# Last-8 keys of a segment packed four heads to a row quadrant, and the output projection in two column halves

## The chip, the cores and the metric

The kernel runs on one core of one Trainium2 chip. The metric is the device time of one execution, in microseconds (us). The engines are named as the profile names them: PE is the matrix engine (PEld its weight loads), DVE the vector engine, ACT the scalar engine, POOL the general engine, SP the engine that issues most DMAs. PSUM is the accumulator memory of PE; it has eight banks of 128 partitions by 2 KB.

## The reference

The model mixes a recurrent attention branch and a small network with a gate. There are 2048 tokens of 512 values, 32 heads of 128, and 64 segments of 32 tokens. Each segment sees 8 memory rows and its own 32 tokens, and the first 8 output rows of a segment are the next segment's memory, so the segments form a chain.

```
for s in range(n_seg):
    h = concatenate([mem, x[:, 32*s:32*s+32]])        # 40 rows
    q, k, v = h@Wq, h@Wk, h@Wv                        # 32 heads of 128
    scores = where(mask, q k^T * scale, -1e9)          # memory rows see all
    o = einsum('bhte,hed->btd', softmax(scores) v, Wo)
    mem = o[:, :8]; outs.append(o[:, 8:])
g = sigmoid((x * gate_w).sum(-1))
return g * a + (1 - g) * (gelu(layernorm(x) @ w1 + b1) @ w2 + b2)
```

## The kernel before

A first stage (lines up to L188) computes the network branch for all tokens and keeps it in SBUF; it ends at about 111 us. After it, a main loop goes over the 64 segments, with two more turns at the end to drain.

**Rows.** PE works on 32 columns of stationary operand at a time, four such quarters beside each other (`tile_position`). A segment has 8 memory rows, 24 tokens that share a quarter with them (the *ride* rows) and the last 8 tokens (the *left* rows). The left rows of four segments, a group T of 128 tokens, are projected together one group ahead: `left_qk` and `left_v` (L265, L276 on the operand `GL`) give `QL`, `KL` and `VL` of a group. Four segments, si = 0 to 3, make a group, and the program repeats with a group's period.

**One turn of the loop**, in PE's order: the q and k projections in five PSUM banks (`qk_unit`, L265 on `hT`), v with one and a half banks (L276), the scores (L413 for 32 keys, L417 for the left keys), the rest of v, the sums of the memory queries' weights (L533, L534), five units of filler, the weighted values of the memory queries, `Um` (L427, L431), the sums of the token queries (L544, L545), two units of filler, the output projection `wo_unit` (L287, 32 matmuls of 512 columns into one bank `wp`), the weighted values of the token queries of the segment before, `Ux` (the same lines L427, L431), a unit of filler, the transposed memory `aT` (L575), the mask of the next segment (L404) and a last unit of filler. The output projection of turn s takes the memory rows of segment s and the ride rows of segment s-2.

**Filler** is the work that no segment waits for at once: `left_qk`, `left_v` of the next group, `wo_left` (the output projection of the left rows), the assembly of the output (L361, L370, L375). A unit is four matmuls of 512 columns or the like, and there are nine a turn.

**Order.** From the first mask on the order is written out by hand (`manual_schedule`): each engine runs its instructions as the loop issues them. DVE and ACT casts that follow filler are put in the lists `dve_q` and `act_q`, and `flush` issues them. Before that point a scheduler orders the work. The seven banks of pool `pb` go round: a new tile waits until the reader of the tile seven allocations before is done. In SBUF, `wsb` (L565, L566) holds the projection of a turn, and `aT` of the next turn reads all of its 512 columns, so the chain of the recurrence is wp, the DVE cast of columns 0 to 255, the ACT cast of columns 256 to 511, aT, `hT` (L576), q.

`ux_out` (L485) casts the four tiles of `Ux` with ACT into `UTT`, whose last axis is the segment in the group, so that each value lands four elements from its neighbour. `Um` lands there by L548, two casts on DVE and two on ACT.

Of the kernel before, what the change touches and what calls it, by code (L numbers as in the profile page):

```python
# [23 lines left out]
def kernel(ctx, tc, A_x, A_mem0, A_Wq, A_Wk, A_Wv, A_Wo, A_seg_len, B_x, B_w1, B_b1, B_w2, B_b2, gate_w, out):  # L24
# [189 lines left out]
    nc.gpsimd.memset(UTT[:], 0.0)  # L214
# [8 lines left out]
    for i in range(SPT):  # L223
        nc.gpsimd.memset(SelL[i][:], 0.0)
        nc.vector.tensor_copy(out=SelL[i][:, RIDE:32], in_=Sel[:, i:32:SPT])
# [3 lines left out]
    for si in range(SPT):  # L229
        for g in range(4):  # L230
            q = slice(32 * g, 32 * g + 32)
            for (c0, c1) in ((0, M), (EW - LEFT, EW)):
                sl = MkA[q, si, c0:c1]
                nc.gpsimd.memset(sl, 0.0)
                nc.gpsimd.affine_select(out=sl, in_=sl, pattern=[[0, c1 - c0]], compare_op=ALU.is_ge,
                                        fill=MASK_NEG, base=-LEFT * si, channel_multiplier=1)
            sl = MkA[q, si, 0:M]
            nc.gpsimd.affine_select(out=sl, in_=sl, pattern=[[0, M]], compare_op=ALU.is_ge,
                                    fill=MASK_NEG, base=LEFT * si + LEFT - 1, channel_multiplier=-1)

            sl = MkA[q, si, EW - LEFT:EW]
            nc.gpsimd.affine_select(out=sl, in_=sl, pattern=[[1, LEFT]], compare_op=ALU.is_ge,
                                    fill=MASK_NEG, base=LEFT * si, channel_multiplier=-1)

            sl = MkA[q, si, 2 * M:2 * M + RIDE]
# [4 lines left out]
    ps = loop.enter_context(tc.tile_pool(name="ps", bufs=1, space=PSUM))  # L250
    cw = loop.enter_context(tc.tile_pool(name="cw", bufs=2))
# [32 lines left out]
    def wo_unit(bk, lhs, u):  # L284
        for (j, i) in HORD[4 * u:4 * u + 4]:
            g = i % 4
            nc.tensor.matmul(bk[32 * g:32 * g + 32, :], lhsT=lhs(i, j), rhs=Wo_sb[:, 4 * i + j, :],  # L287
                             start=(j == 0 and i < 4), stop=(j == 3 and i >= NG - 4), tile_position=(0, 32 * g))

    xTs, GLs, wsbs, wsbLs = {}, {}, {}, {}  # L290
# [30 lines left out]
    def left_qk(T, t, hf):  # L321
        h0, h1 = HF[hf]
        bk = bank([P, 512])
        for kc in range(KC):
            qk_unit(bk, GLs[T], t, h0, h1, kc)
            if kc < KC - 1:
                yield
        dst = (QL, KL)[t][T % 2]

        def ev():  # L330
            nc.gpsimd.tensor_copy(out=dst[:, h0:h1, :], in_=qk_tr(bk, h0, h1))
# [12 lines left out]
    def wo_left(T):  # L344
        bk = bank([P, Dm])
        for u in range(8):
            wo_unit(bk, lambda i, j: UTT[:, i, j, 32:40, :].rearrange("p c i -> p (c i)"), u)
# [32 lines left out]
    def filler(T):  # L380

        if T + 1 < NT:
            for hf in range(2):
                for t in range(2):
                    yield from left_qk(T + 1, t, hf)
            for vb in range(2):
                yield from left_v(T + 1, vb)
        if T >= 1:
            yield from out_units(T - 1)
        elif NT > 2:  # L390
            x_tr(2, x_load(2))
            yield
# [9 lines left out]
    def mask_mm(s):  # L402
        S = ps.tile([P, NG, EW], FP32, tag="S", name="S")
        nc.tensor.matmul(S[:], lhsT=ident[:], rhs=MkA[:, s % SPT, :].unsqueeze(1).to_broadcast([P, NG, EW]),  # L404
# [3 lines left out]
    def scores(S, s, i0, i1):  # L408
        T = s // SPT
        for i in range(i0, i1):  # L410
            for j in range(4):
                h = 4 * i + j
                nc.tensor.matmul(S[32 * j:32 * j + 32, i, M:M + 40], lhsT=KT[:, h, :], rhs=QT[:, h, :],  # L413
                                 start=False, stop=True, skip_group_check=True, tile_position=(0, 32 * j))
            for j in range(4):
                h = 4 * i + j
                nc.tensor.matmul(S[32 * j:32 * j + 32, i, :].rearrange("p (a b) -> p a b", b=8)[:, 0:7:6, :],  # L417
                                 lhsT=KL[T % 2][:, h, :], rhs=QT[:, h, :].rearrange("p (a b) -> p a b", b=8)[:, 0:5:4, :],
                                 start=False, stop=True, skip_group_check=True, tile_position=(0, 32 * j))

    def av(U, n, s, V, Pt, c_main, c_left, u0):

        T = s // SPT
        for i in range(NG):
            for j in range(4):
                q = slice(32 * j, 32 * j + 32)
                nc.tensor.matmul(U[j][:, i, :], lhsT=V[q, i, :], rhs=Pt[q, i, c_main:c_main + n],  # L427
                                 start=(i == 0), stop=False, skip_group_check=True, tile_position=(32 * j, 0))
            for j in range(4):
                q = slice(32 * j, 32 * j + 32)  # L430
                nc.tensor.matmul(U[j][:, i, u0:u0 + 8], lhsT=VL[T % 2][q, i, :], rhs=Pt[q, i, c_left:c_left + 8],  # L431
# [27 lines left out]
    S_next = mask_mm(0)  # L459
    Es, Rs, Pxs, Vs, Uxs = {}, {}, {}, {}, {}  # L460
    fill, left = iter(()), iter(())

    def run_fill(n):
        for _ in range(n):
            if next(left, 0) == 0 and (T + 1 < NT or si >= 2):
                next(fill, None)
# [15 lines left out]
    def ux_out(s):  # L482
        T, si = divmod(s, SPT)
        for j, U in enumerate(Uxs.pop(s)):
            nc.scalar.copy(out=UTT[:, :, j, M:40, si], in_=U[:])  # L485

    for s in range(nseg + 2):
# [5 lines left out]
        if si == 1 and 1 <= T < NT:  # L493
            left = wo_left(T - 1)
        if live:
# [3 lines left out]
            if s >= 1:  # L499
                x_mul(s - 1)  # L500
            flush(dve_q)
            if s + 1 < nseg and (s + 1) // SPT in xTs:
                prep_h(s + 1)
            if s >= 1:
                prep_q(s)
            BANKS = [(0,) + HF[0], (1,) + HF[0], (0,) + HF[1], (1, H // 2, 3 * H // 4), (1, 3 * H // 4, H)]
# [16 lines left out]
            scores(S, s, 0, NG // 2)  # L523
            scores(S, s, NG // 2, NG)
# [22 lines left out]
            for j in range(4):  # L547
                (nc.scalar.copy if j % 2 else nc.vector.tensor_copy)(out=UTT[:, :, j, 0:M, sp], in_=Um[j][:])  # L548
# [16 lines left out]
        nc.vector.tensor_copy(out=wsb[:, 0:256], in_=wp[:, 0:256])  # L565
        nc.scalar.copy(out=wsb[:, 256:512], in_=wp[:, 256:512])  # L566
# [5 lines left out]
        if s + 1 < nseg:  # L572
# [4 lines left out]
            S_next = mask_mm(s + 1)  # L577
        run_fill(1)
        if si == 1:
            for _ in left:  # L580
                pass
# [3 lines left out]
    for _ in wo_left(NT - 1):  # L585
        pass
# [137 lines left out]
```

## Time and profile before

| what | value |
|---|---|
| median of 2 runs | 979.15 us (977.44 to 980.86) |
| the profiled execution | 980.17 us, of which its span is 978.4 us |
| mean granted clock of PE | 0.98 |
| PE busy | 871.1 us (89%) |
| PEld busy | 518.0 us (53%) |
| DVE busy | 514.7 us (53%) |
| ACT busy | 525.9 us (54%) |
| POOL busy | 257.0 us (26%) |

The profile is of one execution. A row of the timeline gives the start in us, the duration in us, engine, line, operation, output and input, the shape, and the count; in brackets is the idle time of that engine just before, with what ended it. A row of the groups gives the busy sum in us and the mean of one in ns, then the idle time before them. Matmuls overlap, so a row of 16 matmuls lasts less than sixteen times the mean of one, and the last one's duration goes on after the next group has begun.

### The profile page before, as it was taken

Reading aid. Unit: us, or ns where it says so; the run is one execution under the profiler, and the core shown is the slowest. Engines: PE = TensorE matmul, PEld = TensorE weight load, DVE = VectorE, ACT = ScalarE, POOL = GpSimd, SP = SyncE. Lnnn points to the kernel's source line nnn. Section 1 sums busy time; section 2 is a strip of 40 time slices with the busy share of each in tenths; the row PEclk is TensorE's granted clock in tenths of the full one; section 3 lists DMA queues with packets and bytes.
Section 4 is the critical chain, followed back from the end, with each engine's and each line's share of the span. In section 5 each row is a group of like instructions: output and inputs, shape, how many; then the busy total and the mean of one; then the engine's idle time right before and its main releaser. Section 6 shows DMA issues by size and latency. Waiting matters only on the chain.

```text
span 978.4 us, 53663 instructions
## 1 busy us (share of the span) xinstructions
PE 871.1 (89%) x24969; PEld 518.0 (53%) x24977; DVE 514.7 (53%) x999; ACT 525.9 (54%) x1252; POOL 257.0 (26%) x599
## 2 busy tenths in 40 slices
PE   2999649998999999999999999989899999999996
PEld 1666315555555555555555555555555555555553
DVE  4721416554556555655565555555555545555553
ACT  2655324555555555555555555555555555555564
POOL 1000463222222232223222223222222222232320
PEclk9999779999999999999999999999999999999999
DMA  9960000000000000000000000000000000000000
GB/s 285 422 199 1 12 2 4 9 4 3 16 4 14 4 15 3 15 4 15 4 15 3 15 4 3 15 4 15 3 15 4 15 4 15 3 9 4 10 7 12
DMA packets 14996, 29.65 MB, mean 30 GB/s; under 512 B 1032, under 2 KB 12656, under 8 KB 13232
## 3 DMA queue, kind: packets, MB, share of 16 engines
q1 hardware_dynamic: 14592, 25.90, 7.4%
q8 instruction: 197, 3.23, 1.4%
q0 software_dynamic: 176, 0.27, 0.3%
q14 instruction: 31, 0.25, 0.1%
HBM read 24.06 MB, written 2.10 MB: 27 GB/s over the span
## 4 chain that ended last, share of the span: by engine, by line
PE 78%; ACT 11%; DVE 4%; issue 3%; POOL 2%; DMA 1%; SPq 1%; POOLq 0%; ACTq 0%; DVEq 0%
PE b L265 29%; PE b L287 16%; PE b L276 11%; ACT UTT L485 4%; PE b L427 4%; PE bp L172 4%; PE hp L178 3%; PE b L431 3%; ACT E L530 2%; DVE wsb L565 2%; ACT wsb L566 2%; PE S L417 2%; PE S L413 2%; PE b L533 1%; PE b L544 1%
## 5 line engine op out<-in xcount | busy, mean ns | idle before, releaser
L271 DVE STREAM_TRANSPOSE Tt<-b 128x512 f32<-128x512 f32 (+1 forms) x384 | 225.6, 613 | 111.3 <-PE b L265 82.7
L265 PEld LDWEIGHTS <-hT 128*32 128x32 bf16 x5120 | 144.3, 98 | 111.1 <-issue 14.4
L485 ACT CAST UTT<-b 128x256 bf16<-128x256 f32 x256 | 158.3, 822 | 10.8 <-PE b L431 10.5
L287 PE MATMUL b<-Wo_sb,UTT 128*32 128x512 bf16 x2624 | 161.5, 383 | 2.3 <-ACT UTT L485 1.6
L265 PE MATMUL b<-Wq_sb,hT 128*32 128x512 bf16 x2048 | 137.2, 388 | 18.7 <-POOL hT L396 13.5
L265 PE MATMUL b<-Wk_sb,hT 128*32 128x256 bf16 (+1 forms) x3072 | 137.4, 313 | 0.0
L276 PE MATMUL b<-Wv_sb,hT 128*32 128x512 bf16 x2048 | 134.5, 380 | 0.0
L472 POOL TENSOR_TENSOR Px<-E,R 128x256 bf16<-128x256 bf16 x64 | 43.2, 675 | 345.2 <-DVE R L549 345.2
L513 ACT CAST KT<-Tt 128x256 bf16<-128x256 f32 (+1 forms) x192 | 86.8, 476 | 57.4 <-DVE Tt L271 57.4
L549 DVE RECIPROCAL R<-b 128x256 f32<-128x256 f32 x64 | 112.0, 1750 | 4.5 <-PE b L545 4.5
L566 ACT CAST wsb<-b 128x256 bf16<-128x256 f32 x66 | 24.6, 373 | 157.7 <-DVE wsb L565 157.7
L287 PEld LDWEIGHTS <-UTT 128*32 128x32 bf16 x2624 | 73.0, 106 | 62.4 <-ACT UTT L485 3.5
L427 PEld LDWEIGHTS <-V 32*128 32x128 bf16 x4096 | 68.0, 91 | 58.1 <-DVE Pm L539 29.5
L537 DVE RECIPROCAL R<-b 128x64 f32<-128x64 f32 x64 | 35.7, 558 | 96.6 <-PE b L534 96.6
L513 POOL CAST QT<-Tt 128x512 bf16<-128x512 f32 x64 | 39.4, 616 | 172.4 <-DVE Tt L271 172.4
L431 PEld LDWEIGHTS <-VL 32*128 32x128 bf16 x4096 | 69.1, 91 | 13.4 <-issue 13.3
L548 ACT CAST UTT<-b 128x64 bf16<-128x64 f32 x128 | 28.5, 319 | 79.8 <-PE b L431 79.8
L276 PEld LDWEIGHTS <-hT 128*32 128x32 bf16 x2048 | 53.5, 96 | 25.9
L513 ACT CAST QT<-Tt 128x512 bf16<-128x512 f32 x64 | 39.6, 618 | 50.0 <-DVE Tt L271 49.4
L178 PE MATMUL hp<-yT,w_sb 128*128 128x256 bf16 (+1 forms) x352 | 53.0, 278 | 4.8 <-ACT hTm L179 3.1
L548 DVE CAST UTT<-b 128x64 bf16<-128x64 f32 x128 | 28.4, 301 | 54.0 <-PE b L431 54.0
L179 ACT ACTIVATE hTm<-hp,b_sb 128x256 bf16<-128x256 f32 (+1 forms) x88 | 40.6, 470 | 29.9 <-PE hp L178 29.8
(111 smaller groups left out, 1271.4 us busy)
## 6 DMA issues: line engine op xcount, KB each, us to landing
Wq_sb<-in_A_Wq_dram SPq DMA_DIRECT2D x4, 1024.0 KB, 13.0
Wk_sb<-in_A_Wk_dram SPq DMA_DIRECT2D x4, 1024.0 KB, 18.7
Wv_sb<-in_A_Wv_dram SPq DMA_DIRECT2D x4, 1024.0 KB, 20.2
Wo_sb<-in_A_Wo_dram SPq DMA_DIRECT2D x4, 1024.0 KB, 17.2
out_dram<-o SPq DMA_DIRECT2D x16, 128.0 KB, 1.7
xc<-in_A_x_dram SPq DMA_DIRECT2D x15, 128.0 KB, 2.3
x_all<-in_A_x_dram SPq DMA_DIRECT2D x3, 512.0 KB, 9.2
w_sb<-in_B_w_dram SPq DMA_DIRECT2D x1, 1376.0 KB
```

The costliest lines, as they stand in the source:

```text
L178: nc.tensor.matmul(hp[:rows, :], lhsT=w1_sb[:, kc, fc * P:fc * P + rows], rhs=yT[:, kc, :], start=(kc == 0), stop=(kc == KC - 1))
L265: nc.tensor.matmul(bk[32 * j:32 * j + 32, 0:n], lhsT=G[:, kc, :], rhs=W5[t][:, kc, h0:h1, j, :], start=(kc == 0), stop=(kc == KC - 1), til ...
L271: nc.vector.transpose(out=Tt[:, 0:n], in_=bk[:, 0:n])
L276: nc.tensor.matmul(bk[32 * j:32 * j + 32, :], lhsT=G[:, kc, :], rhs=Wv5[:, kc, 4 * vb:4 * vb + 4, j, :], start=(kc == 0), stop=(kc == KC - ...
L287: nc.tensor.matmul(bk[32 * g:32 * g + 32, :], lhsT=lhs(i, j), rhs=Wo_sb[:, 4 * i + j, :], start=(j == 0 and i < 4), stop=(j == 3 and i >= ...
L427: nc.tensor.matmul(U[j][:, i, :], lhsT=V[q, i, :], rhs=Pt[q, i, c_main:c_main + n], start=(i == 0), stop=False, skip_group_check=True, til ...
L431: nc.tensor.matmul(U[j][:, i, u0:u0 + 8], lhsT=VL[T % 2][q, i, :], rhs=Pt[q, i, c_left:c_left + 8], start=False, stop=True, skip_group_che ...
L485: nc.scalar.copy(out=UTT[:, :, j, M:40, si], in_=U[:])
L513: (nc.gpsimd.tensor_copy if bi == 2 else nc.scalar.copy)(out=dst, in_=Tv)
L548: (nc.scalar.copy if j % 2 else nc.vector.tensor_copy)(out=UTT[:, :, j, 0:M, sp], in_=Um[j][:])
L549: nc.vector.reciprocal(out=R[:, 8 * NG:].rearrange("p (i q) -> p i q", q=32), in_=sr[:])
L566: nc.scalar.copy(out=wsb[:, 256:512], in_=wp[:, 256:512])
```

## The change

**Left keys.** Before, each of the 32 heads has a matmul of its own for the left keys: the stationary operand is the 32 left keys of all four segments for this head, of which the mask lets 8 count. Afterwards the stationary operand holds the 8 left keys of this segment for four heads (`KL` in the order group of heads, segment, head, key), and the moving operand the two query blocks of the four heads, so that 8 matmuls of 64 columns stand for 32 of 16. Of the result only the blocks with query and key of the same head count; `MkA` masks the others and is now the same for all segments, so `mask_mm` takes no segment. The values follow: `VL` has the rows of four heads in a quarter, and in `Um` and in `Ux` 8 matmuls of 32 columns stand for 32 of 8. Main and left matmuls no longer alternate: the left ones come after all main ones.

**Values through DRAM.** The left values are cast by ACT into `vt`, written to a DRAM tile in two DMAs of a group, and read back by 16 DMAs, all issued by SP. `KL` is written by POOL in two casts of 128x256 for each bank in place of one of 128x512. `left_v` is moved ahead of `left_qk` in the filler, and `wo_left`, which had a list of its own that began in the second segment, is put behind `left_qk`.

**Output projection.** `UTT` becomes two tiles, one for even and one for odd groups, in which a value's neighbours lie beside each other: segment si uses columns 24-8si to 64-8si, and its left rows end up in columns 32 to 63. `wo_unit` runs twice over 256 columns, into two banks; DVE casts the first half between the two in program order, and ACT the second.

**Small moves.** POOL does `prep_h` and `prep_q` ahead of `x_mul`, and the flush of `dve_q` follows. The memset of `UTT` covers 2048 columns in place of 5120, and 32 small memsets of `MkA` are gone.

```diff
-    KL = [lp.tile([P, H, 32], BF16, name=f"KL{i}") for i in range(2)]
-    VL = [lp.tile([P, NG, Dh], BF16, name=f"VL{i}") for i in range(2)]
-    UTT = lp.tile([P, NG, 4, 40, SPT], BF16)
-    MkA = lp.tile([P, SPT, EW], BF16)
+    KL = [lp.tile([P, 8, SPT, 4, LEFT], BF16, name=f"KL{i}") for i in range(2)]
+    VL = [lp.tile([P, SPT, 2, Dh], BF16, name=f"VL{i}") for i in range(2)]
+    UTT = [lp.tile([P, NG, 4, 64], BF16, name=f"UTT{i}") for i in range(2)]
+    MkA = lp.tile([P, 4, EW], BF16)
...
-    nc.gpsimd.memset(UTT[:], 0.0)
+    nc.gpsimd.memset(UTT[1][:], 0.0)
...
-    def wo_unit(bk, lhs, u):
+    def wo_unit(bk, ut, c0, u, d0=0, d1=Dm):
         for (j, i) in HORD[4 * u:4 * u + 4]:
             g = i % 4
-            nc.tensor.matmul(bk[32 * g:32 * g + 32, :], lhsT=lhs(i, j), rhs=Wo_sb[:, 4 * i + j, :],
+            nc.tensor.matmul(bk[32 * g:32 * g + 32, :], lhsT=ut[:, i, j, c0:c0 + 32], rhs=Wo_sb[:, 4 * i + j, d0:d1],
...
+            if t == 0:
+                nc.gpsimd.tensor_copy(out=QL[T % 2][:, h0:h1, :], in_=Tv)
+            else:
+                for hh in range(h0 // 8, h1 // 8):
+                    r0 = 8 * hh - h0
+                    nc.gpsimd.tensor_copy(out=KL[T % 2][:, :, :, hh, :], in_=Tv[:, r0:r0 + 8, :].rearrange("p g (s c) -> p g s c", c=LEFT))
...
-        act_q.append(lambda: nc.scalar.copy(out=v_out(VL[T % 2], vb), in_=bk[:]))
+        def ev():
+            vt = cw.tile([P, 4, Dh], BF16, tag="vt", name="vt")
+            nc.scalar.copy(out=vt[:].rearrange("p i e -> p (i e)"), in_=bk[:])
+            if vb == 0:
+                vds[T] = dr.tile([P, 4, 2, Dh], BF16, tag="vd", name="vd")
+            nc.sync.dma_start(vds[T][:, 2 * vb:2 * vb + 2], vt[:].rearrange("p (a g) e -> p a g e", g=2))
+            if vb == 1:
...
+                for j in range(4):
+                    for hh in range(4):
+                        r0 = 32 * j + LEFT * hh
+                        nc.sync.dma_start(VL[T % 2][r0:r0 + LEFT].rearrange("p s g e -> p s (g e)"), src[j, hh])
...
-    def scores(S, s, i0, i1):
+    def scores(S, s):
...
+        for g in range(2):
             for j in range(4):
...
-                                 lhsT=KL[T % 2][:, h, :], rhs=QT[:, h, :].rearrange("p (a b) -> p a b", b=8)[:, 0:5:4, :],
+                                 lhsT=KL[T % 2][:, 4 * g + j, si, :, :].rearrange("p h c -> p (h c)"),
+                                 rhs=QT[:, 4 * g + j:H:8, :].rearrange("p h (a b) -> p h a b", b=8)[:, :, 0:5:4, :],
...
+        for g in range(2):
             for j in range(4):
                 q = slice(32 * j, 32 * j + 32)
-                nc.tensor.matmul(U[j][:, i, u0:u0 + 8], lhsT=VL[T % 2][q, i, :], rhs=Pt[q, i, c_left:c_left + 8],
+                nc.tensor.matmul(U[j][:, g:NG:2, u0:u0 + 8], lhsT=VL[T % 2][q, si, g, :], rhs=Pt[q, g:NG:2, c_left:c_left + 8],
...
-            nc.scalar.copy(out=UTT[:, :, j, M:40, si], in_=U[:])
+            nc.scalar.copy(out=UTT[T % 2][:, :, j, c0 + M:c0 + 40], in_=U[:])
...
-        wp = bank([P, Dm])
-        for u in range(8):
-            wo_unit(wp, lambda i, j: UTT[:, i, j, 0:32, sp], u)
-        flush(act_q, 2)
         wsb = cw.tile([P, Dm], BF16, tag="wsb", bufs=7, name="wsb")
-        nc.vector.tensor_copy(out=wsb[:, 0:256], in_=wp[:, 0:256])
-        nc.scalar.copy(out=wsb[:, 256:512], in_=wp[:, 256:512])
+        for half in range(2):
+            d = slice(256 * half, 256 * half + 256)
+            wp = bank([P, 256])
+            for u in range(8):
+                wo_unit(wp, UTT[Tp % 2], 24 - 8 * sp, u, 256 * half, 256 * half + 256)
+            if half == 0:
+                flush(act_q, 2)
+            (nc.scalar.copy if half else nc.vector.tensor_copy)(out=wsb[:, d], in_=wp[:])
```

The rows that follow are from the program's own order, of one engine each; in brackets are the engines that an instruction waits for, and the numbers behind a name tell tiles of one pool apart.

PE at the end of the output projection of a third segment (si = 2), before: `b_15386` is the bank of the projection, `b_15424` to `b_15427` are the four tiles of `Ux`.

```order
L287 MATMUL b_15386<-Wo_sb_61,UTT_1153 32x512
L427 LDWEIGHTS V_14720
L427 MATMUL b_15424<-Px_15063,V_14720 128x32
L427 LDWEIGHTS V_14720
L427 MATMUL b_15425<-Px_15063,V_14720 128x32 [waits Activation_49]
L427 LDWEIGHTS V_14720
L427 MATMUL b_15426<-Px_15063,V_14720 128x32 [waits DVE_49]
L427 LDWEIGHTS V_14720
L427 MATMUL b_15427<-Px_15063,V_14720 128x32 [waits Activation_49]
L431 LDWEIGHTS VL1_1152
L431 MATMUL b_15424<-Px_15063,VL1_1152 128x8
L431 LDWEIGHTS VL1_1152
```

The same place on PE afterwards: `b_14407` is the bank of the second half, `b_14441` to `b_14444` are the tiles of `Ux`.

```order
L291 MATMUL b_14407<-Wo_sb_61,UTT1_1154 32x256
L451 LDWEIGHTS V_13769
L451 MATMUL b_14441<-Px_14092,V_13769 128x32
L451 LDWEIGHTS V_13769
L451 MATMUL b_14442<-Px_14092,V_13769 128x32 [waits DVE_49]
L451 LDWEIGHTS V_13769
L451 MATMUL b_14443<-Px_14092,V_13769 128x32 [waits DVE_49]
L451 LDWEIGHTS V_13769
L451 MATMUL b_14444<-Px_14092,V_13769 128x32 [waits Activation_49]
L451 LDWEIGHTS V_13769
```

The second half of the projection stands directly ahead of `Ux`, the left matmuls have left the space between the main ones, and the fourth tile of `Ux` now follows an ACT reader of a half's bank rather than the reader of the whole.

ACT at the same two places. Before, `b_15302` and `b_15304` are tiles of `Um`, `wsbL` is the projection of the left rows, `wsb` that of the turn:

```order
L548 CAST UTT_1153<-b_15302 128x8x8 [waits PE_49]
L548 CAST UTT_1153<-b_15304 128x8x8 [waits PE_49]
L353 CAST wsbL_15419<-b_14831 128x512
L566 CAST wsb_15421<-b_15386 128x256 [waits DVE_49]
L485 CAST UTT_1153<-b_15424 128x8x32 [waits PE_49]
L485 CAST UTT_1153<-b_15425 128x8x32 [waits PE_49]
L485 CAST UTT_1153<-b_15426 128x8x32 [waits PE_49]
L485 CAST UTT_1153<-b_15427 128x8x32 [waits PE_49]
```

And afterwards, where `b_14407` is the second half:

```order
L570 CAST UTT1_1154<-b_14312 128x8x8 [waits PE_49]
L570 CAST UTT1_1154<-b_14314 128x8x8 [waits PE_49]
L590 CAST wsb_14372<-b_14407 128x256 [waits PE_49]
L511 CAST UTT1_1154<-b_14441 128x8x32 [waits DVE_49,PE_49,Activation_49]
L511 CAST UTT1_1154<-b_14442 128x8x32 [waits PE_49,Activation_49]
L511 CAST UTT1_1154<-b_14443 128x8x32 [waits DVE_49,PE_49]
L511 CAST UTT1_1154<-b_14444 128x8x32 [waits PE_49,Activation_49]
```

The ACT cast of `wsb` waited for DVE, which cast the other columns of the same bank first, and now waits for PE alone; the cast of `wsbL` has moved to another segment.

POOL just ahead of the loop, before (the copy of the first group's `GL` stands 80 rows earlier, directly behind the memset of `MkA`):

```order
L235 AFFINE_SELECT MkA_1154<-MkA_1154 32x8 [waits Pool_49] x2
L314 COPY GL_1493<-xT_1491 128x128 [waits DVE_49,Pool_49]
L238 AFFINE_SELECT MkA_1154<-MkA_1154 32x8 [waits Pool_49]
L242 AFFINE_SELECT MkA_1154<-MkA_1154 32x8
L238 AFFINE_SELECT MkA_1154<-MkA_1154 32x8
L242 AFFINE_SELECT MkA_1154<-MkA_1154 32x8
L235 AFFINE_SELECT MkA_1154<-MkA_1154 32x8 x2
L396 COPY hT0_1142<-xT_1480 128x4x24 [waits Pool_49]
L396 COPY hT1_1143<-xT_1480 128x4x24
```

And afterwards:

```order
L245 AFFINE_SELECT MkA_1155<-MkA_1155 32x8 [waits Pool_49]
L241 AFFINE_SELECT MkA_1155<-MkA_1155 32x8 [waits Pool_49]
L245 AFFINE_SELECT MkA_1155<-MkA_1155 32x8 [waits Pool_49]
L318 COPY GL_1453<-xT_1451 128x128 [waits DVE_49,Pool_49]
L419 COPY hT0_1142<-xT_1451 128x4x24
L419 COPY hT1_1143<-xT_1451 128x4x24
L318 COPY GL_1464<-xT_1462 128x128 [waits DVE_49]
L335 CAST QL0_1147<-Tt_1484 128x512 [waits DVE_49]
L339 CAST KL0_1149<-Tt_1504 128x32x8 [waits DVE_49]
```

Both copies of `GL` and those of `hT` now stand behind the last of `MkA`'s selects, which before lay partly behind the first and the second.

More of the change, by code (lines that the diff above doesn't have):

```diff
@@ L224 @@
         nc.gpsimd.memset(SelL[i][:], 0.0)
-        nc.vector.tensor_copy(out=SelL[i][:, RIDE:32], in_=Sel[:, i:32:SPT])
+        nc.vector.tensor_copy(out=SelL[i][:, RIDE:32], in_=Sel[:, LEFT * (SPT - 1 - i):LEFT * (SPT - i)])
     nc.gpsimd.memset(MkA[:], 0.0)
-    for si in range(SPT):
+    for hh in range(4):
         for g in range(4):
@@ L382, in filler @@
         if T + 1 < NT:
+            for vb in range(2):
+                yield from left_v(T + 1, vb)
             for hf in range(2):
@@ L385, in filler @@
                     yield from left_qk(T + 1, t, hf)
-            for vb in range(2):
-                yield from left_v(T + 1, vb)
         if T >= 1:
+            yield from wo_left(T - 1)
             yield from out_units(T - 1)
@@ L522 @@
                 v_unit(vb1, hc, 1, kc)
[L523 to L524 removed]
+            scores(S, s)
             for kc in range(2, KC):
@@ L576 @@
             nc.vector.tensor_copy(out=hn[:, :, 0:M], in_=aT[:])
-            S_next = mask_mm(s + 1)
+            S_next = mask_mm()
         run_fill(1)
-        if si == 1:
-            for _ in left:
-                pass
         if si == SPT - 1:
```

57 lines of the change are left out of this document (27 added, 30 removed).

## The prediction

> **What bounds the kernel now.** I read the page first, for the busy shares and the chain that ended last.
>
> ```profile
> span 978.4 us, 53663 instructions
> PE 871.1 (89%) x24969; PEld 518.0 (53%) x24977; DVE 514.7 (53%) x999; ACT 525.9 (54%) x1252; POOL 257.0 (26%) x599
> PE 78%; ACT 11%; DVE 4%; issue 3%; POOL 2%; DMA 1%; SPq 1%; POOLq 0%; ACTq 0%; DVEq 0%
> ```
>
> PE holds 78% of the chain, ACT and DVE 15% between them: less PE work and shorter hand-overs can both count. Next the windows of one group of four segments, from mask to mask (columns: us, then busy us of each engine, granted clock).
>
> ```profile
> 500.38:551.73 51.35, 48.28 (x1525) 28.74 (x1523) 29.01 (x54) 29.08 (x72) 14.47 (x29) 1.00 0.03 9
> 229.40:234.60 5.20, 5.20 (x88) 2.66 (x84) 2.55 (x5) 2.21 (x4) 1.17 (x3) 0.67 0.01 3
> ```
>
> A group takes 51.35 us, of which PE is idle for 3.07. The second row is one of three spots with a low clock. Then the timeline of a first segment (si = 0) of that group, into the second.
>
> ```profile
> 500.92 1.05 PE L265 MATMUL b<-Wq_sb,hT 128*32 128x512 bf16 x16 [0.18 <-ACT UTT L485]
> 501.78 1.05 PE L265 MATMUL b<-Wk_sb,hT 128*32 128x512 bf16 x16
> ...
> 503.50 1.06 PE L265 MATMUL b<-Wk_sb,hT 128*32 128x256 bf16 x32
> 504.38 1.48 PE L276 MATMUL b<-Wv_sb,hT 128*32 128x512 bf16 x24
> ...
> 505.53 0.58 ACT L519 CAST V<-b 128x512 bf16<-128x512 f32 x1
> 505.67 0.21 PE L413 MATMUL S<-QT,KT 128*32 128x40 bf16 x4
> ...
> 506.17 0.62 PE L276 MATMUL b<-Wv_sb,hT 128*32 128x512 bf16 x8
> 506.50 0.28 ACT L530 ACTIVATE E<-S 128x128 bf16<-128x128 f32 x1 [0.39 <-PE S L417]
> ...
> 508.26 0.18 PE L427 MATMUL b<-Pm,V 32*128 32x8 bf16 x4
> ...
> 508.70 0.20 PE L431 MATMUL b<-Pm,VL 32*128 32x8 bf16 x4
> 508.97 0.45 DVE L548 CAST UTT<-b 128x64 bf16<-128x64 f32 x2 [0.85 <-PE b L431]
> 509.51 1.90 PE L287 MATMUL b<-Wo_sb,UTT 128*32 128x512 bf16 x32
> 511.46 0.42 DVE L565 CAST wsb<-b 128x256 bf16<-128x256 f32 x1 [0.47 <-PE b L287]
> 511.92 0.37 ACT L566 CAST wsb<-b 128x256 bf16<-128x256 f32 x1 [2.46 <-DVE wsb L565]
> 512.19 2.47 ACT L485 CAST UTT<-b 128x256 bf16<-128x256 f32 x4
> 512.35 0.24 PE L575 MATMUL b<-Sel,wsb 128*128 128x8 bf16 x4
> 512.45 0.35 PE L404 MATMUL S<-MkA,ident 128*128 128x448 bf16 x1
> 512.99 0.40 PE L265 MATMUL b<-Wq_sb,GL 128*32 128x512 bf16 x4 [0.19 <-ACT UTT L485]
> 513.55 1.05 PE L265 MATMUL b<-Wq_sb,hT 128*32 128x512 bf16 x16 [0.17 <-ACT UTT L485]
> ```
>
> The chain of the recurrence runs through every row: scores, exponentials (ACT waits for the last score), Um, its casts, the projection, the DVE cast, then the ACT cast in series, aT, mask, q. Whatever PE does less of ahead of a hand-over shortens the turn. The third segment (si = 2) ends worse:
>
> ```profile
> 534.77 1.90 PE L287 MATMUL b<-Wo_sb,UTT 128*32 128x512 bf16 x32
> 536.73 0.42 DVE L565 CAST wsb<-b 128x256 bf16<-128x256 f32 x1 [0.53 <-PE b L287]
> 537.18 0.37 ACT L566 CAST wsb<-b 128x256 bf16<-128x256 f32 x1 [2.57 <-DVE wsb L565]
> 537.61 0.17 PE L427 MATMUL b<-Px,V 32*128 32x32 bf16 x1 [0.81 <-ACT wsb L566]
> 538.29 2.46 ACT L485 CAST UTT<-b 128x256 bf16<-128x256 f32 x4 [0.74 <-PE b L431]
> 539.07 0.24 PE L575 MATMUL b<-Sel,wsb 128*128 128x8 bf16 x4 [0.53 <-ACT UTT L485]
> ```
>
> Here the fourth tile of Ux waits for the bank of the projection, and aT for the bank of Ux's first tile: 2.40 us from the projection's end (536.67) to aT, against 0.94 in the first segment (511.41 to 512.35).
>
> **The change part by part**, per group of four segments. The groups by form give the durations that the timeline lacks (busy sum in us, mean in ns).
>
> ```profile
> L485 ACT CAST UTT<-b 128x256 bf16<-128x256 f32 x256 | 158.3, 822 | 10.8 <-PE b L431 10.5
> L566 ACT CAST wsb<-b 128x256 bf16<-128x256 f32 x66 | 24.6, 373 | 157.7 <-DVE wsb L565 157.7
> L287 PEld LDWEIGHTS <-UTT 128*32 128x32 bf16 x2624 | 73.0, 106 | 62.4 <-ACT UTT L485 3.5 <-issue 1.7 <-DVE UTT L548 1.6
> ```
>
> *Scores.* 64 matmuls take 505.67 to 506.17, 0.50 us, 7.8 ns each, so the 32 left ones cost 0.25. Eight of 64 columns replace them. By issue they cost 8 × 7.8 = 0.06; by columns too, since the projection's 512 columns take 1.90/32 = 59 ns, which makes 7.4 ns for 64. Gain 0.18 a turn, 0.72 a group. The bound on the other side is nothing: if their scattered columns cost 31 ns each, or if ACT, which has the V cast until 506.11, is late instead.
>
> *Um.* 60 starts from 508.26 to 508.70 give 7.3 ns a matmul; 24 go, 0.17 a turn, 0.68 a group, on the path since the L548 casts and the projection follow at once. Ux loses 24 as well, which counts below.
>
> *Projection in halves.* No row has narrow projection matmuls; the nearest is K with 256 columns: 32 of them, weight loads included, take 503.50 to 504.38, 0.88 us, against 0.86 for 16 of 512 (500.92 to 501.78). Doubling the loads costs 0.02 per 32, so 0.04 a turn, +0.16 a group. In K's rows the four quarters in a row load the same hT columns, as the projection's do not, so the other bound is a rival below.
>
> The Trainium skill, "TensorE: Matmul & The Clock Gate", section "The mechanism", says that a weight load overlaps running matmuls only where its row group differs, and here all loads use all rows; its section "LDWEIGHTS (loading the stationary operand)" gives columns/1.2 ns, an estimate of 27 ns for 32 columns. By that page the 32 added loads cost 0.85 a turn and the sum ends near 983; K's 27.5 ns for load and matmul together speak against it.
>
> *Hand-over of wsb, si = 0 and 3.* DVE's 0.42 and the 0.04 behind it leave the path, since DVE casts the first half while PE does the second; at most 0.46. PE itself still has Ux (shorter by 0.17) and a filler unit (0.21 of PE's time by 0.86/4) ahead of aT, so I take 0.30, twice: 0.60.
>
> *si = 2.* The fourth tile of Ux now waits for ACT's half alone. After the projection's end: ACT 0.06 + 0.37, then 0.06 to PE, 0.49; the rest of Ux, now 537.61 to 538.25 or 0.64, less 0.19, 0.94; the first Ux cast 0.04 + 0.37 + 0.06, 1.41 in place of 2.40. Gain 1.0, if that cast takes what ACT takes for a 128x256 tile into neighbouring columns (L566, 373 ns) and not the 822 of L485, whose target had a stride of four. With the old 0.78 it is 1.76: gain 0.64.
>
> The Trainium skill, "SBUF — State Buffer", section "Door 1: The DMA port swizzle (why `[64,N]` ≈ `[32,N]`)", says that two hits per 16-byte line give full bandwidth, so bf16 may stride by up to 8 for free; by that rule L485 would gain nothing. The two rows of the trace, 822 against 373 for like tiles from PSUM, speak against it but differ in more than the stride.
>
> *si = 1.* In the changed program aT waits here for Ux's first tile, as si = 2 did: 0.42 for ACT's half, 0.47 for the cast, 0.9 in all, against 0.94 now; nothing, or +0.3 with slow casts. Its q projection starts 1.10 after the mask (512.45 to 513.55) against 0.54 in the first segment, behind L485; with four casts in some 1.5 in place of 2.47 I take 0.45 of the 0.56. The wait of the token sums for an Um cast moves from si = 2 to si = 1, at no change.
>
> *Values through DRAM.* 18 DMAs a group on SP, whose queue is otherwise stores and loads of x. left_v comes first in the filler, so they have three segments, some 38 us. Hidden. POOL's extra casts lie in its 37 idle us of 51.
>
> *Start.*
>
> ```profile
> 111.23 4.37 POOL L214 MEMSET UTT<- 128x5120 bf16 x1 [106.62 <-ACT c_all L188]
> 117.48 0.14 POOL L234 MEMSET MkA<- 32x8 bf16 x2
> 117.59 1.90 PE L265 MATMUL b<-Wq_sb,GL 128*32 128x512 bf16 x16 [3.22 <-POOL MkA L234]
> 124.39 0.35 PE L404 MATMUL S<-MkA,ident 128*128 128x448 bf16 x1
> 138.24 1.90 PE L265 MATMUL b<-Wq_sb,hT 128*32 128x512 bf16 x16 [13.49 <-POOL hT L396]
> 138.61 0.19 POOL L242 TENSOR_SCALAR_AFFINE_SELECT MkA<-MkA 32x8 bf16<-32x8 bf16 x1
> 144.39 0.19 PE L413 MATMUL S<-QT,KT 128*32 128x40 bf16 x4
> ```
>
> GL now comes after all of MkA's selects, the last of which ended at 138.80. But the memset of UTT is shorter by 4.37 × 3/5 = 2.6, 16 pairs of small memsets go (0.14 and a start each, some 3.5), and GL and hT (some 0.8) no longer stand between. POOL reaches GL at about 131.9, an estimate; PE then does the left projections (117.59 to 124.39, 6.8), and q starts near 138.6, but without the idle 13.49 ahead of it: 4.75 to the first score (500.92 to 505.67), not 6.15. So 0 to −1; with the tail, −0.5.
>
> The sum per group: −0.72 − 0.68 + 0.16 − 0.60 − 1.0 − 0.45 = −3.29. PE's busy 48.28 falls by some 1.9, so the new group of 48.06 still has 1.7 idle. Over 15.5 groups (16, the first without the two-turn lag) that is −51. The profiled execution took 980.17: 980.2 − 51 − 0.5 = 928.7, and the median lies 1.0 below the profiled one: 928.
>
> **The rivals.** *The casts of Ux stay slow.* Then si = 2 gains 0.64, si = 1 loses 0.3, q gains nothing: −2.18 a group, −34, some 945. For it: the tiles are the same size; against it: row L566.
>
> *The waits only move.* ACT is busy with V until 506.11 and the scores gain nothing, the hand-overs of si = 0 and 3 end on PE's filler, and the casts stay slow: −0.68 + 0.16 + 0.3 − 0.64 = −0.86, −13, some 965: no change. Against it: ACT waits 0.39 for the scores at 506.50.
>
> *Weight loads set the pace of the halves: slower.* If a narrow pair takes what a wide one takes, 59 ns, the projection doubles: +1.9 in each of 66 turns, +125 on 928, so 1051 with the 0.04 taken off. From 24 ns per added pair (51/2112) the change loses. For it: the loads' mean of 106 ns; against it: K's 27.5 ns a pair.
>
> *Weight loads are laid bare, but only just.* The 2624 loads are busy for 73.0, 27.8 ns each; 32 more a turn at that price on the path are 0.89, +59 over 66 turns: 985, no change.
>
> *More than forecast.* All terms at their best give about −4.2 a group, and the low-clock spots (1.7 us each) may go: 980.2 − 65 − 5 − 2 = 908.
>
> **The numbers.** Forecast 0.47, slow casts 0.23, moved waits 0.11, more 0.10, loads as pace 0.06, loads laid bare 0.03. A measurement tells 2% from no change, that is 959.6 and 998.7. Faster: the forecast, slow casts and more, 0.80; same, the moved waits and the loads laid bare, 0.14; slower 0.06. The range from 910 to 960 holds the three faster cases.
>
> **What would show it.** L485's successor near 400 ns (else the second case); L431's successor with a quarter of the matmuls and scores to v in 0.32; the projection's 64 in 1.9 to 2.0 (a rival, if 2.5 or more); ACT's wsb cast waiting for PE; aT in a third segment 1.4 after the projection. The forecast is wrong if the group's period stays above 50, or if a row shows PE waiting for VL's DMAs.

## The result, and the profile after

The changed kernel takes 920.57 us (918.77 to 922.37) against 979.15: a ratio of 0.940, interval 0.930 to 0.951. That is faster, as forecast; the forecast was 928 with a range from 910 to 960. The profiled execution took 922.37, with a span of 920.6.

The page of the changed kernel, busy shares and the chain that ended last:

```profile
span 920.6 us, 49285 instructions
PE 832.7 (90%) x22481; PEld 519.9 (56%) x22481; DVE 502.2 (55%) x999; ACT 443.2 (48%) x1252; POOL 257.1 (28%) x599
PE 81%; ACT 7%; issue 3%; DVE 3%; DMA 2%; POOL 2%; SPq 1%; ACTq 0%; POOLq 0%; DVEq 0%
```

ACT's share of the chain fell from 11% to 7%, its busy time by 83 us; PE's busy time fell by 38. A group of four segments, mask to mask, in the windows (us, then busy us of each engine):

```profile
429.25:477.00 47.75, 45.99 (x1364) 28.53 (x1363) 28.35 (x54) 23.95 (x72) 14.80 (x32) 1.00 0.07 21
```

The group went from 51.35 to 47.75, by 3.60 where 3.29 was forecast, and PE's idle time in it from 3.07 to 1.76 (1.7 forecast). The end of a third segment, in the timeline, answers to the rows that showed 2.40 us from projection to aT before:

```profile
463.32 0.36 DVE L590 CAST wsb<-b 128x256 bf16<-128x256 f32 x1
463.78 0.19 PE L451 MATMUL b<-Px,V 32*128 32x32 bf16 x3
463.90 0.37 ACT L590 CAST wsb<-b 128x256 bf16<-128x256 f32 x1 [2.16 <-PE b L291]
464.32 0.35 PE L451 MATMUL b<-Px,V 32*128 32x32 bf16 x29 [0.35 <-ACT wsb L590]
464.86 1.20 ACT L511 CAST UTT<-b 128x256 bf16<-128x256 f32 x4 [0.59 <-PE b L456]
465.29 0.24 PE L599 MATMUL b<-Sel,wsb 128*128 128x8 bf16 x4 [0.20 <-ACT UTT L511]
```

DVE casts its half while PE still works, ACT waits for PE alone, the fourth tile of Ux comes at 464.32, and aT at 465.29: 1.45 after the projection's end (about 463.84, the 0.06 ahead of ACT's start taken off), where 1.41 was forecast. The groups by form, projection and casts:

```profile
L291 PE MATMUL b<-Wo_sb,UTT 128*32 128x256 bf16 x4224 | 130.7, 278 | 1.1 <-ACT UTT L511 0.8
L511 ACT CAST UTT<-b 128x256 bf16<-128x256 f32 x256 | 77.0, 387 | 12.8 <-PE b L456 10.0
```

The Ux casts take 387 ns in place of 822. What went worse stands in a first segment (si = 0), and far ahead of it on SP's queue:

```profile
450.65 6.09 SPq L361 DMA_DIRECT2D VL<-vd  x16
...
484.57 0.36 PE L451 MATMUL b<-Pm,V 32*128 32x8 bf16 x32
484.79 0.81 PE L456 MATMUL b<-Pm,VL 32*128 32x32 bf16 x8
486.22 1.92 PE L291 MATMUL b<-Wo_sb,UTT 128*32 128x256 bf16 x64
```

Eight left matmuls take 0.81 there and 0.23 in the other segments, though the last of the reads that they need had been issued 28 us before. And the start:

```profile
131.15 1.90 PE L269 MATMUL b<-Wq_sb,GL 128*32 128x512 bf16 x16
138.66 1.03 PE L269 MATMUL b<-Wq_sb,hT 128*32 128x512 bf16 x16
142.38 5.50 SPq L361 DMA_DIRECT2D VL<-vd  x16
149.35 0.20 PE L456 MATMUL b<-Pm,VL 32*128 32x32 bf16 x5 [1.26 <-DMA VL<-vd]
...
150.68 3.02 PE L291 MATMUL b<-Wo_sb,UTT 128*32 128x256 bf16 x64
```

q starts at 138.66 (138.6 forecast), but the first VL is late: SP needs 5.50 us to issue 16 reads, and PE waits for the last of them. That is the row of PE waiting for VL's DMAs which the prediction had named as a sign that it is wrong; it stands in the first group alone. And the first projection behind it takes 3.02 us in place of 1.92, because the granted clock fell. The window of the low clock (0.53, behind POOL's column):

```profile
149.35:152.75 3.40, 3.40 (x55) 2.08 (x59) 2.20 (x4) 0.82 (x3) 0.88 (x2) 0.53 0.11 39
```

### The profile page after: what moved, and what is told of

It reads as the page before. It is cut to its first block, busy times and chain, and to the rows that moved or that the text cites. A ratio compares the mean times of both kernels' runs of the same rounds, so it can differ in the third digit from the quotient of the medians.

```text
span 920.6 us, 49285 instructions
## 1 busy us (share of the span) xinstructions
PE 832.7 (90%) x22481; PEld 519.9 (56%) x22481; DVE 502.2 (55%) x999; ACT 443.2 (48%) x1252; POOL 257.1 (28%) x599
## 4 chain that ended last, share of the span: by engine, by line
PE 81%; ACT 7%; issue 3%; DVE 3%; DMA 2%; POOL 2%; SPq 1%; ACTq 0%; POOLq 0%; DVEq 0%
PE b L269 32%; PE b L291 16%; PE b L280 12%; PE b L451 4%; PE bp L172 3%; PE hp L178 3%; ACT E L552 3%; PE b L456 2%; PE S L436 2%; PE b L566 1%; ACT wsb L590 1%; PE b L599 1%; PE b L555 1%; ACT UTT L511 1%; PE S L427 1%
## 5 line engine op out<-in xcount | busy, mean ns | idle before, releaser
L269 PEld LDWEIGHTS <-hT 128*32 128x32 bf16 x5120 | 134.1, 97 | 93.1 <-DVE hT L600 6.3
L291 PE MATMUL b<-Wo_sb,UTT 128*32 128x256 bf16 (+1 forms) x4736 | 166.4, 289 | 1.1 <-ACT UTT L511 0.8
L291 PEld LDWEIGHTS <-UTT 128*32 128x32 bf16 x4736 | 125.3, 98 | 26.9 <-issue 3.1
L269 PE MATMUL b<-Wq_sb,hT 128*32 128x512 bf16 x2048 | 132.9, 379 | 1.3
L269 PE MATMUL b<-Wk_sb,hT 128*32 128x256 bf16 (+1 forms) x3072 | 133.3, 308 | 0.0
L511 ACT CAST UTT<-b 128x256 bf16<-128x256 f32 x256 | 77.0, 387 | 12.8 <-PE b L456 10.0
L280 PEld LDWEIGHTS <-hT 128*32 128x32 bf16 x2048 | 50.7, 96 | 28.2
L451 PEld LDWEIGHTS <-V 32*128 32x128 bf16 x4096 | 36.2, 91 | 50.8 <-DVE Pm L561 29.0
L600 DVE CAST hT<-b 128x32 bf16<-128x32 f32 x63 | 12.0, 191 | 90.3 <-PE b L599 90.3
L570 ACT CAST UTT<-b 128x64 bf16<-128x64 f32 x128 | 20.9, 215 | 77.5 <-PE b L456 77.5
L499 POOL TENSOR_TENSOR racc<-racc,R 128x320 f32<-128x320 f32 x64 | 55.1, 862 | 0.0
```

The source lines that it names most:

```text
L269: nc.tensor.matmul(bk[32 * j:32 * j + 32, 0:n], lhsT=G[:, kc, :], rhs=W5[t][:, kc, h0:h1, j, :], start=(kc == 0), stop=(kc == KC - 1), til ...
L280: nc.tensor.matmul(bk[32 * j:32 * j + 32, :], lhsT=G[:, kc, :], rhs=Wv5[:, kc, 4 * vb:4 * vb + 4, j, :], start=(kc == 0), stop=(kc == KC - ...
L291: nc.tensor.matmul(bk[32 * g:32 * g + 32, :], lhsT=ut[:, i, j, c0:c0 + 32], rhs=Wo_sb[:, 4 * i + j, d0:d1], start=(j == 0 and i < 4), stop ...
L499: nc.gpsimd.tensor_tensor(out=racc[:], in0=racc[:], in1=R[:], op=ALU.add)
L511: nc.scalar.copy(out=UTT[T % 2][:, :, j, c0 + M:c0 + 40], in_=U[:])
```

## The experiments

Beside these runs the kernel before took 979.9 to 980.6 us. Differences are against the 920.6 us of the changed kernel unless said otherwise. "A group" is the mask-to-mask time of four segments, as the sum of the medians of each segment.

**One bank for the projection.**

```diff
-        for half in range(2):
-            wp = bank([P, 256])   ... 64 matmuls of 256 columns
+        wp = bank([P, Dm])        ... 32 matmuls of 512 columns
+        nc.vector.tensor_copy(out=wsb[:, 0:256], in_=wp[:, 0:256])
+        nc.scalar.copy(out=wsb[:, 256:512], in_=wp[:, 256:512])
```

> The changed kernel with the output projection again in one bank of 512 columns, cast by DVE and then by ACT; all else as changed. Hand-over theory (the DVE cast beside PE's second half is worth what the prediction says): the DVE cast comes back into the path, 0.30 in si = 0 and 3, some 0.46 in si = 2 and 0.2 in si = 1, less 0.04 a turn for the halves, so about 1.1 us a group of 47.7, +17 us, some 938. Rival (the gain came from the faster casts of Ux and from fewer matmuls, the halves are beside the path): within 6 us of 920.6.

Measured: 939.4 us, +18.8, as the hand-over theory has it. The third segment's end in this kernel's timeline:

```profile
469.72 0.42 DVE L587 CAST wsb<-b 128x256 bf16<-128x256 f32 x1 [0.48 <-PE b L291]
470.18 0.37 ACT L588 CAST wsb<-b 128x256 bf16<-128x256 f32 x1 [2.60 <-DVE wsb L587]
470.61 0.35 PE L451 MATMUL b<-Px,V 32*128 32x32 bf16 x29 [0.81 <-ACT wsb L588]
```

The wait of the fourth Ux tile is back to 0.81 from 0.35. The halves are worth their hand-over. The group went from 47.7 to 49.0.

**UTT with its old stride.**

```diff
-    UTT = [lp.tile([P, NG, 4, 64], BF16, name=f"UTT{i}") for i in range(2)]
+    UTT = [lp.tile([P, NG, 64, 4], BF16, name=f"UTT{i}") for i in range(2)]
```

> The changed kernel with UTT's last two axes exchanged, so that a value's neighbours in a cast lie four elements apart as before the change; size, order and waits are unchanged. Stride theory: the Ux casts go back from 387 to about 820 ns, which costs 0.36 in si = 2, 0.3 in si = 1 and 0.45 ahead of q, 1.1 a group, +17 us, some 938. Rival (the rule that two hits in a 16-byte line are enough, so the stride was free and something else made the casts faster): casts stay near 390 ns and the time at 920.

Measured: 940.9 us, +20.3. Its group of Ux casts:

```profile
L511 ACT CAST UTT<-b 128x256 bf16<-128x256 f32 x256 | 158.5, 818 | 12.1 <-PE b L456 9.2
```

Nothing but the place of neighbours was changed, and the casts doubled. The stride of four bf16 is the whole difference between 387 and 818 ns. PE's weight loads read the same tile at that stride, but the projection takes as long as before (1.85 us to the first Ux matmul in both), so the time was lost at the casts.

**Left keys unpacked.** Scores, `av`, `KL`, `VL`, `left_v` and the mask as before the change; the rest as changed.

> The changed kernel with the left keys and values unpacked again: 32 left matmuls each in scores, Um and Ux, VL written by ACT without DRAM, a mask for each segment; contiguous UTT, halves and the order of POOL stay. Theory (removed matmuls lie on the path): scores +0.21 and Um +0.19 a turn, 1.6 a group, less the 0.58 that the first left matmuls of a group now take in si = 0 and some 2 us at the start: +1.0 a group, +14 us in all, some 935. Rival (the matmuls were hidden, waits only move): within 5 us of 920.6, or below it, since the wait of si = 0 goes too.

Measured: 959.6 us, +39, well above the 14 expected. Two things were left out of that expectation. Ux's 24 more matmuls lie ahead of aT as well: by the medians, scores cost 0.8 a group more, Ux to aT 0.85, Um to Ux 0.2, or 28 us over 15.5 groups. And PE now stops at irregular places, with no wait that the profile shows (the releaser "issue"). The largest of them in the timeline:

```profile
489.00 0.40 PE L374 MATMUL b<-wsbL,SelL 128*32 128x512 bf16 x4 [1.05 <-issue]
```

From 160 us on there are 24 such stops, 10.1 us together, against 2 and 0.5 us in the changed kernel and 6 and 1.7 us in the kernel before. The start went the other way: without the trip through DRAM the first turn, from the loop's first q to the second mask, takes 12.0 us in place of 15.6.

**A relay for VL.** From the second group on the 16 reads land in a tile that POOL copies to VL.

```diff
-                        nc.sync.dma_start(VL[T % 2][r0:r0 + LEFT]...
+                        nc.sync.dma_start((VR if T else VL[0])[r0:r0 + LEFT]...
...
+            if si == SPT - 1 and T + 1 < NT:
+                nc.gpsimd.tensor_copy(out=VL[(T + 1) % 2][:], in_=VR[:])
```

> The changed kernel with the 16 reads of a group landing in a relay tile that POOL copies into VL in the group's last segment, from the second group on; PE's first left matmuls of a group then wait for POOL alone and not for 15 DMA semaphores. Theory (the 0.58 us in si = 0 is the cost of the many satisfied waits on PE, since the reads landed 28 us before): the eight left matmuls of Um take 0.24 in si = 0 as in the other segments, -0.55 a group, -8 us, some 912. Rival (it is something else in si = 0, the data or the banks): 920, and the eight still take 0.8.

Measured: 908.9 us, -11.6. A first segment in its timeline:

```profile
477.80 0.23 PE L457 MATMUL b<-Pm,VL 32*128 32x32 bf16 x8
```

0.23 in place of 0.81; si = 0 went from 11.90 to 11.32, which makes 9 us. In the changed program four weight loads of PE wait for three or four DMA semaphores each, 14 waits in all, and the reads had raised them long before; in the trace these four loads start 0.13 to 0.26 us apart, and the four without waits 3 to 4 ns apart. The relay takes the waits off PE and the 0.58 goes with them, some 0.15 us for each of the four loads.

The first turn, which still reads VL straight from the DMAs, was 2.2 us shorter here than in the changed kernel. PE waits for the reads in both (0.83 us for the last of them here), but here the clock did not fall behind the wait: the projection takes 1.92, not 3.02, and the token sums to the second mask 3.14, not 4.77.

**Quarters.**

```diff
-                wo_unit(wp, UTT[Tp % 2], 24 - 8 * sp, u, 256 * half, 256 * half + 256)
+            for qt in range(2):  ... the same for 128 columns
```

> The changed kernel with each half of the output projection done as two quarters of 128 columns in the same bank: 128 matmuls and weight loads a turn in place of 64, same columns, same banks, same casts. Theory (columns set the pace; the scores' pairs of load and 40 columns ran at 7.8 ns, all rows, so a load of 32 columns is cheap): the projection stays at 1.9 to 2.1 us, time 920 to 935, the upper part if the larger number of PE instructions brings the irregular issue stalls that the unpacked kernel shows (25 of them, 10 us). Rival (loads are laid bare once the columns are few, 27 ns each): 128 x 27 = 3.5 us, +1.6 a turn, some 1020.

Measured: 980.6 us, +60, which neither expectation has. Two turns in its timeline:

```profile
495.13 1.46 PE L291 MATMUL b<-Wo_sb,UTT 128*32 128x128 bf16 x91
497.59 0.73 PE L291 MATMUL b<-Wo_sb,UTT 128*32 128x128 bf16 x37 [1.00 <-issue]
...
520.18 1.96 PE L291 MATMUL b<-Wo_sb,UTT 128*32 128x128 bf16 x128
```

Where PE isn't stopped, 128 matmuls of 128 columns take 1.96, as 64 of 256 do (1.92): weight loads do not set the pace, and the rival of 1020 is out. But 48 stops of issue from 160 us on make 41.5 us, where the expectation had 10 in its upper part. Another 2.5 us are the 0.04 a turn, and three more spots of low clock in the loop cost about 5; the remaining 10 or so are not placed.

**Narrow q and v.**

```diff
-                           rhs=Wv5[:, kc, 4 * vb:4 * vb + 4, j, :]      # 512 columns
+        for a in (0, 2):   rhs=Wv5[:, kc, 4 * vb + a:4 * vb + a + 2, j, :]   # 256; q alike
```

> The changed kernel with q's two banks and v's two, of the segments and of the left rows, done in matmuls of 256 columns in place of 512: some 64 more pairs of load and matmul a turn, as many as the quarters added, but with the columns that K's rows show to be harmless (0.02 us per 32 pairs, so 0.05 a turn, +3 us); the projection stays in halves. Theory (PE runs out of instructions once a turn holds some 890 of them in 12 us, whatever they are): irregular issue stalls of 0.2 to 2 us at places other than the split ones as well, 10 to 45 us in all, 933 to 968. Rival (it was the 128-column projection itself): no issue stalls, 921 to 926.

Measured: 940.7 us, +20, as the theory has it. There are stops at other lines too, 28 of them with 10.3 us, which is half of the loss; 3 more were expected for the columns, and the rest is not placed. The waits of PE, grouped (us in total, times, longest):

```profile
PE b L454 <- issue: 3.7, 9, 0.8
PE b L459 <- issue: 2.4, 7, 0.8
PE b L283 <- issue: 1.8, 4, 0.7
PE b L271 <- issue: 1.6, 5, 0.5
```

L454 and L459 are Um and Ux, which were not touched. So the stops come with the number of instructions, not with one kind: in kernels with 45,000 to 53,700 recorded instructions they make 0 to 1.7 us, in those with 57,700 to 59,500 they make 10 to 42, most where 256 of PE's instructions stand in 1.9 us.

The traces also show what these stops wait for. Each page lists a DMA queue q8 of the kind "instruction", 178 packets in the changed kernel and 210 to 218 in the three with many stops, and the trace has the time of every packet (16 KB, about 1 us each). There is one packet for some 253 matmuls and weight loads, in this kernel as in the others, so the queue brings PE its program. Of the 100 stops in these three kernels, 98 end between 1.15 and 1.65 us after a packet of that queue has ended. Of moments taken at random 13% do so, and of PE's other waits in these kernels 26 of 177. So PE stops until its next instructions have arrived. What holds the queue up is not shown.

**POOL's order as before.**

```diff
             if s >= 1:
-                prep_q(s)
                 x_mul(s - 1)
             flush(dve_q)
+            prep_h, prep_q behind the flush
```

> The changed kernel with POOL's order and the flush of the DVE list ahead of q as before: x_mul, flush, prep_h, prep_q. Theory (the shorter wait ahead of q came from the casts of Ux, POOL's order is beside the path): within 4 us of 920. Rival (hT's and QT's left columns came late behind x_mul, and the order is part of the gain): 0.1 to 0.5 a turn longer from mask to scores, 927 to 950.

Measured: 920.8 us, +0.2. The order is beside the path.

**Both hand-over edits undone.** One bank and the old stride together.

> The changed kernel with both edits of the one-bank and the stride run undone at once: the projection in one bank, UTT's neighbours four elements apart; packed left keys, DRAM trip, POOL's order and the start stay. Theory (the two parts of the hand-over, wsb's cast and the Ux casts, lie one after the other on the same path, so their losses add): 920.6 + 18.8 + 20.3, some 960, so that packing by itself is worth some 20 us and not the 39 that its removal cost. Rival (they overlap, one hides behind the other): 945 or less.

Measured: 968.6 us (961.5 to 969.4), +48 in place of the 39 that the two cost singly. The group, by the medians, is no worse than the two together make it: +2.3, against 1.3 and 1.1. The difference lies in the clock. Windows of this kernel (clock behind POOL's column): the end of a third segment, and the projections after it.

```profile
476.50:479.70 3.20, 1.84 (x65) 1.03 (x57) 0.76 (x2) 1.25 (x3) 1.75 (x3) 1.00 0.03 5
479.70:485.00 5.30, 5.30 (x81) 2.40 (x83) 2.52 (x5) 2.58 (x5) 0.61 (x1) 0.68 0.01 2
```

PE is busy for 1.84 of 3.20 us, and then the granted clock is 0.68 and q to the first score takes 6.1 in place of 4.76. This kernel has that six times between 160 and 920 us, always behind a third segment, 9 us in all. The kernel before has it three times in that place, 5 us in all, and neither the changed kernel nor the two with a single edit undone has it there once. (Elsewhere in the loop the kernel before has one more spot of low clock, at 185.5, and the changed one has one at 869.7, in the last group, where PE has no filler.) The same stretch in both, before first:

```profile
226.00:229.30 3.30, 1.97 (x85) 1.17 (x81) 0.75 (x3) 1.75 (x4) 1.74 (x3) 1.00 0.00 0
```

```profile
462.00:465.30 3.30, 2.74 (x113) 2.17 (x106) 1.68 (x2) 0.81 (x3) 1.75 (x3) 1.00 0.02 5
```

60% busy before, 83% after. That share is the same behind nearly every third segment of a kernel, so the low clock follows only some of the stretches that are busy for 60%: 3 of 14 in the kernel before, 6 of 14 in this one.

**Three small steps on the relay kernel.** First, the first group's `left_v` ahead of its `left_qk`.

> The relay kernel with the first group's left_v ahead of its left_qk, so that the DRAM trip of the first VL starts some 4 us earlier. Theory (the 2 us by which the first turn is later than forecast are the first VL: the 16 reads issue in 5.5 us of SP and land at 149.3, while PE reached them at 147.2): the wait for VL in the first Um goes, about -2 us against the relay kernel, 907. Rival (first turn late for another reason): 909, and PE still waits after 147.

Measured: 906.8 us, -2.2 against the relay kernel, where -2 was expected. But the wait for the first VL gave only 0.7 of that, the second mask came 1.0 earlier, and the two profiled executions have the same span, 906.6. The wait is gone; what that is worth lies within the spread of the runs.

Then one more flush:

```diff
             (nc.scalar.copy if half else nc.vector.tensor_copy)(out=wsb[:, d], in_=wp[:])
+            if half == 0:
+                flush(dve_q)
```

> The kernel with relay and early left_v, and one flush of the DVE list right behind the DVE cast of the first half, so that a finished left q or k bank is transposed, and free, before Ux and aT ask for a bank. By the build, aT of si = 1 and 2 then follows ACT's half of wsb and no longer the first Ux cast. Theory (what is left of the si = 2 wait is a shortage of banks): Ux to aT falls from 1.50 to about 0.75 in si = 2 and from 0.94 to 0.72 in si = 1, -1.0 a group, -15 us, some 892. Rival (the transpose delays the DVE cast of hT, or the fourth Ux tile's wait grows by as much): 905 or more.

Measured: 902.2 us, -4.6 where -15 was expected. Ux to aT fell from 1.50 to 1.25 in si = 2 and from 0.94 to 0.85 in si = 1: PE now waits 5.4 us in all for DVE's transpose itself, which frees the bank.

Last, an exponential of one column ahead of the loop.

> The kernel with relay, early left_v and the early flush, and one exponential of a single column ahead of the loop, so that ACT loads the table while PE does the first left projections. Theory: the 1.28 us table load leaves the first turn, -1 us, some 901. Rival: another load of a table follows, 902 or more.

Measured: 900.0 us (899.5 to 903.3), a ratio of 0.919 to the kernel before, interval 0.916 to 0.922. That is the best version here. In the first turn the first score to the sums went from 2.15 to 0.98, so the table load has left it; in the whole time this last step is within the noise.

## Why the prediction was right, and where not

*Scores and Um.* Forecast 0.18 and 0.17 a turn; first score to sums went from 1.25 to 1.04, Um to the token sums, where nothing else waits, from 0.57 to 0.38. Right, and that the matmuls lay on the path is shown by the unpacked run: both go back to 1.24 and 0.57.

*Projection in halves.* 1.92 for 64 against 1.90 for 32: +0.02 where +0.04 was forecast. The rule of "TensorE: Matmul & The Clock Gate" (the Trainium skill, section "The mechanism"), by which the added loads would show, does not hold here: 128 loads with all rows in 1.96 us (the quarters run) leave 15 ns for load and matmul together.

*Hand-over, si = 0 and 3.* Ux to aT went from 1.00 to 0.72, 0.28 where 0.30 was taken. *si = 2:* 2.46 to 1.50, 0.96 against 1.0. *si = 1:* 1.00 to 0.94, as said. *Ahead of q in si = 1:* 1.10 to 0.51, 0.59 against 0.45 taken from an upper bound of 0.56; that si = 0 gained 0.11 there too was not in the sum.

*The casts.* Row L566 was the right guide: 387 ns. The rival "the casts of Ux stay slow" falls. The rule of "SBUF — State Buffer" (the Trainium skill, section "Door 1: The DMA port swizzle (why `[64,N]` ≈ `[32,N]`)"), by which a stride of four bf16 is free, does not hold for these casts: it cost ACT a factor of two.

*Values through DRAM: "Hidden."* This step failed. From the second group on the transfers are hidden, but the waits for their semaphores are not: 0.58 a group on PE, 9 us in all. The step had no term for them.

*Start.* "0 to −1" failed too: the second mask came at 154.26 in place of 152.05, +2.2. The loop's first q was where it was forecast, and q to the first score took 4.76, as said. Left out was that 16 reads issue one after the other on SP, 0.34 us each, so that PE waits for VL. The first turn is 3.6 us longer than in the unpacked run, which has no such reads: 2.0 at VL's matmuls, and 1.6 behind them in the low clock.

*Low-clock spots.* They were named in a rival only. The three behind third segments went, some 5 us, because the hand-over shortened the idle stretch ahead of them; the run with both hand-over edits undone brought them back. (The prediction counts three such spots; the loop of the kernel before has four, the fourth elsewhere.)

The sum: the loop from the second mask to the last went from 799.74 to 740.50, -59.2, of which 15.5 groups at 3.60 make -55.8 and the clock much of the rest; the start +2.2; what follows the last mask -0.8. That is -57.8 in the span, where -51.5 was forecast. The group's terms, 0.31 too small each time, make 4.8 of the miss.

That the sum came so close is in part luck, since these 0.31 are the difference of two larger misses. VL's waits, which had no term, cost 0.58. Against them stand gains of some 0.9 that were not forecast: 0.3 ahead of q, 0.3 ahead of Ux in si = 3 (a filler unit there had waited for ACT's Um cast, and no longer does), 0.2 in scores and Um, 0.1 in the projection, and 0.1 in the wait of the token sums, which moved from si = 2 to si = 1 as said, but not at no change (0.53 less, 0.43 more). The relay kernel, in which "hidden" holds but for the first group, took 908.9, which lies just below the forecast's range.

The single undoings add to 78 us, more than the 58.6 of the change: packing costs 39 where it is taken away last, and gains 12 where it stands alone (980.5 to 968.6). The runs show about where those 27 lie. With the wsb casts in series, Ux to aT in a fourth segment is 1.00 with and without packing, since the cast ends last; with the halves it is 0.98 without and 0.72 with. Over all segments, from Ux to the next q, packing takes 1.0 off a group with the halves and the new stride and 0.1 without them, and the difference makes 14 us. The stops of issue in the unpacked kernel are 10, of which the other kernels have next to nothing (1.7 in the kernel before), and the low clock takes 4 more from the packed kernel with slow hand-overs than from the kernel before.

## What to carry to other kernels

Cost a change on the engine that waits by the row of the wait, and then ask what else the change issues there: satisfied DMA semaphores on PE, DMA issues in a row on SP and added instructions each had a price that no busy share showed. Splitting a result by columns into two banks, so that its cast runs beside the second half, paid here because the chain waited for that cast. The target's stride belongs to the price of a cast.

## What was not expected of the hardware

- Waits of PE that had long been satisfied cost 0.58 us for 14 waits on DMA semaphores at four weight loads (0.81 against 0.23 us); through one POOL copy they cost PE nothing.
- PE stopped for its own instructions in the three kernels with 57,700 to 59,500 of them: 10.1, 41.5 and 10.3 us, against 0 to 1.7 in those with up to 53,700. Of these stops 98 in 100 ended 1.15 to 1.65 us after a packet on the instruction queue.
- The granted clock fell to about 0.7 behind stretches of some 3.2 us in which PE was busy for 57 to 60%, with no single gap over 0.81 us; not at each of them (3 of 14 and 6 of 14), and not where it was busy for 83%. The Trainium skill, "TensorE: Matmul & The Clock Gate", section "What's actually happening", has the clock fall after an idle window of some 3.4 us; here a window that was little more than half busy was enough, which agrees better with that page's section "A second HAM failure mode: psum-queue depth-cycling", on short idle times between groups of matmuls.
